# All eight accumulator banks as one set, in attention and in the MLP, with other durations in the planner

## The chip, the cores and the metric

The kernel runs on one core of one Trainium2 chip. The metric is the device time of one execution in microseconds; it is given as the median of several runs. One further execution was recorded by the hardware profiler, and every duration below comes from that recording.

Five engines work side by side: PE (TensorE, the matrix engine, with its weight loads shown as PEld), DVE (VectorE), ACT (ScalarE), POOL (GpSimd) and SP (SyncE, which here only issues DMAs). Each takes its own instructions in the order in which the program lists them. PE writes its results into accumulator banks (PSUM); there are eight of them, each 512 float32 wide on 128 partitions. DVE and ACT empty a bank; POOL works on SBUF only.

## The reference, cut to what matters

Attention over 4 batches, 8 heads, 768 positions, 64 dimensions: only pairs whose hash buckets agree take part (the signs of six random projections give the bucket), and the output feeds an MLP with a spatial gate.

```python
q_bucket = sum((q @ proj > 0) * 2**bit);  k_bucket likewise
scores   = where(q_bucket == k_bucket, q @ k.T / 8, -1e9)
attn     = exp(scores - max);  attn /= attn.sum() + 1e-9
x        = (attn @ v), heads side by side          # (4, 768, 512)
h        = gelu_tanh(x @ w_in);  u, v = halves of h # 512 wide each
v        = layer_norm(v) * g_ln
gated    = u * (w_sg @ v + b_sg)                   # w_sg mixes positions
out      = x + gated @ w_out
```

All products are float32; most are made of three or four reduced-precision products of a high and a low part.

## The kernel before

**Attention** runs over 16 pairs of heads; both heads of a pair stand on the two halves of the partitions. For each pair the program transposes q and k (`parts`, L476), projects them (`features`, L498), takes the row maxima of the scores (`largest`, product L518, maximum on DVE L525), turns the maxima into a shift (`shift`, DVE L533 and L534, product L540), and then, for each half of the positions, goes three times over two key tiles (`weigh`): scores L562, exponentials on ACT L568, their product with v L574 into one accumulator tile `av`, and running sums on POOL L583. `finish` adds the sums up over the partitions with a product against ones (L599), copies `av` out, and scales through small DMAs; its last DVE step is L620 and its result goes to DRAM as `xs`.

**The MLP** runs over four batches. For each: `hidden_v` (six tiles of 128 positions, product L757 in four groups of three matmuls each, then a chain of ACT and DVE steps L741 to L773), `hidden_u` (eight tiles, product L789, likewise four groups each, DVE L742 and L746), `gate` (eight tiles, product L807 in six groups each, DVE L810 and L814, ACT L815, POOL L818) and `project` (six tiles, product L833 in four groups each and a residual L838, copied out by ACT L842). In the first batch come `gate_weights`, twelve transposes of w_sg (PE L716, ACT L722, DVE L725), and `out_weights`: 16 jobs of seven DVE steps (L357 to L366) that make a high and a low part of w_out. The first `project` needs all sixteen. A "group" below is what the planner places as one piece: two matmuls of a pair of heads and more in attention, three matmuls in the MLP.

**What sets the order.** `Plan` holds a list of pieces of work with an engine, an assumed duration, a priority and the buffers they read and write. `order` runs through them once, at build time, with these assumed durations, and lists for each engine which piece comes after which. The chip then runs each engine's list in that order, whatever the true durations are. On PE the plan adds `TURN_PE` when the form of the array changes: "row" is a pair of products with 64 rows each (L518, L562), "col" a pair with 64 columns each (L574), None the full array.

**The banks.** In attention seven banks (`g0` to `g6`, `ps_tile`) are handed out by the planner, whichever is free first; the eighth is a ring of one, `av`. For `hidden_v` of the first batch the same seven are used. Then both pools are closed and the MLP has three rings: four banks `h` (hidden_v, hidden_u and the transposes of w_sg), two banks `vs` (gate), two banks `o` (project). A ring is used in turn: the fifth `h` tile waits until the first one has been read for the last time, which for hidden_v and hidden_u is DVE L746.

```python
ps_slots = {i: 0.0 for i in range(8 - NAV)}
st.av = ps_t.ring([P, 512], F32, "av", NAV)
return (po_ if tag == "o" else pm).ring(list(shape), F32, "ps_" + tag, bufs)
```

Of the kernel before, what the change touches and what calls it, by code (L numbers as in the profile page):

```python
# [24 lines left out]
AVP = 3.75  # L25
NAV = 1
# [7 lines left out]
class Plan:  # L34
# [8 lines left out]
    TURN_PE = 0.09  # L43
# [59 lines left out]
    def order(self):  # L103
# [120 lines left out]
def kernel(  # L224
# [179 lines left out]
    ps_t, ps_s = Pool("ps_t", "left", PSUM), Pool("ps_s", "left", PSUM)  # L404
    ftp = ps_t.pool.tile([P, 512], F32, tag="av", name="ftp", bufs=NAV)
# [12 lines left out]
    if True:  # L418
# [3 lines left out]
        ps_slots = {i: 0.0 for i in range(8 - NAV)}  # L422
# [14 lines left out]
        NPT = 16  # L437
# [29 lines left out]
        def parts(st, s, prio):  # L467

            hh, lo, raw, fac = st.hi[s], st.lo[s], st.raw[s], (SCALE, 1.0)[s]
            for hf in range(2):  # L470
# [19 lines left out]
        def features(st, s, prio):  # L490
            hh, lo, ft = st.hi[s], st.lo[s], st.ft[s]
            for hf in range(2):
# [11 lines left out]
                plan.add(PE, 0.58, prio, project, [(hh, hf), (lo, hf), (ft, hf)], [fp])  # L504
                plan.add(DVE, 0.67, prio, sign, [fp], [(ft, hf)])

        def largest(st, t, prio):
# [13 lines left out]
            for kh in range(2):  # L521
                plan.add(PE, 0.36, prio + 0.01 * kh, lambda kh=kh: mm(kh),
                         [(st.hi[0], hf), (st.hi[1], kh), (st.ft[0], hf), (st.ft[1], kh)], sc[kh], form="row")
                for j in range(2):
                    plan.add(DVE, 0.56, prio, lambda j=j, kh=kh: nc.vector.tensor_reduce(  # L525
                        mx()[:, kh, i, j:j + 1], sc[kh][j]()[:, :SH], axis=AX.X, op=ALU.max, negate=True),
                        [sc[kh][j]], [(mx, (kh, j, i))])
# [20 lines left out]
        def weigh(st, hf, k0, prio):  # L548

            cs, two = slice(hf * SH, (hf + 1) * SH), (k0, k0 + 1)  # L550
            if k0 == 0:
                st.av = ps_t.ring([P, 512], F32, "av", NAV)
                st.sum = [late.ring([P, SH], F32, "sum", 4) for _ in range(2)]
            av, sums = st.av, st.sum
# [16 lines left out]
            def product():
                for i, kt in enumerate(two):
                    for j in range(2):
                        nc.tensor.matmul(av()[row(j), :SH + 1], st.v()[:, j, kt, :], p[i][j](), start=(kt == 0), stop=(kt == NT - 1))  # L574

            plan.add(PE, 1.48, prio + AVP, product, p[0] + p[1] + [st.v], [av], form="col")
            for i, kt in enumerate(two):
# [3 lines left out]
                for j in range(2):  # L581
                    def add(j=j, i=i, e=e, first=p[0][j] if kt == 1 else sums[j]):
# [3 lines left out]
                             [sums[j]], port=True)  # L586

        def finish(st, hf, prio):
# [12 lines left out]
            plan.add(PE, 0.6, prio, total, sums, [tp])  # L601
# [50 lines left out]
        for n in range(NPAIR):  # L652
            for c in range(NT):
# [28 lines left out]
    def load_x(b, prio):  # L682
        r = []
        for c in range(NC):
# [7 lines left out]
            plan.add(ACT, 0.73, prio + c, lambda x=x, xh=xh: nc.scalar.copy(xh(), x()), [x], [xh])  # L692
            plan.add(M_["xl"], 1.76 if M_["xl"] == POOL else 0.87, prio + c, low, [x, xh], [xl])
# [9 lines left out]
    def gate_weights(prio):  # L703

        sg_v = w_sg.rearrange("(p t) s -> t p s", t=NT)
        for t in range(NT):
# [30 lines left out]
    def gelu2(ps, dst, n, prio, key=None):  # L737

        h2 = tile_of([P, FH], F32, "h2", 2)
        us = n / 960.0  # L740
        plan.add(ACT, us - 0.02, prio, lambda: nc.scalar.activation(h2()[:, :n], ps()[:, :n], AF.Square), [ps], [h2])  # L741
        plan.add(DVE, us + 0.07, prio, lambda: nc.vector.scalar_tensor_tensor(  # L742
            h2()[:, :n], h2()[:, :n], 1.0 / GA, ps()[:, :n], op0=ALU.add, op1=ALU.mult), [h2, ps], [h2])
        plan.add(ACT, us - 0.02, prio, lambda: nc.scalar.activation(h2()[:, :n], h2()[:, :n], AF.Tanh, scale=GC * GA),
# [4 lines left out]
    def hidden_v(xx, prio):  # L749
        zh, zl = tile_of([P, NT, FH], F32R, "zh", 1), tile_of([P, NT, FH], F32R, "zl", 1)  # L750
        for t in range(NT):
            ps, p0 = ps_of("h", 4), prio + t
            ts_ = slice(t * P, (t + 1) * P)
            for c, (xh, xl) in enumerate(xx):
# [4 lines left out]
                plan.add(PE, 0.65, p0 + 0.01 * c, mm, [xh, xl], [ps])  # L759
# [4 lines left out]
            plan.add(DVE, 0.6, p0, lambda y=y, st=st: V.bn_stats(st(), y()), [y], [st])  # L764
# [140 lines left out]
```

## Time and profile before

| what | value |
|---|---|
| time, three runs | 828.22, 830.72, 831.31 us |
| span of the profiled execution (first to last instruction) | 829.1 us |
| PE busy | 795.1 us, 96 % of the span, 5480 matmuls |
| DVE busy | 602.3 us, 73 % |
| POOL, ACT busy | 449.5 us, 54 %; 415.3 us, 50 % |
| granted clock of PE, mean | 0.988 |
| 16 DMA engines, mean | 74 GB/s |

The profiled execution is one more execution of the same program; its own time is its span, 829.1 us, which lies between the lowest run and the median. Attention fills the first 484 us, the MLP the rest. A page of the profile gives busy times per engine, then the same in 40 slices, the chain of work that ended last, and groups of equal instructions; other views show the waits, single instructions in order of time, and busy times in chosen stretches.

### The profile page before, as it was taken

What the parts mean: (1) busy time and instruction counts of PE and PEld (TensorE: products, weight loads), DVE (VectorE), ACT (ScalarE), POOL (GpSimd) and SP (SyncE); (2) the same over time, 40 slices, a digit from 0 to 9 for tenths busy, and PEclk for the clock granted to TensorE, in tenths of its full rate; (3) what the DMA queues carried; (4) which work ended last, traced back from release to release, by engine and by line L of the source; (5) the groups of instructions that cost most, each with busy time, mean ns of one, the idle gap of its engine ahead of it and who ended that gap; (6) DMA issues with size and microseconds to landing.
All of it is one profiled execution on the core that took longest, in us unless ns stands there. A gap on an engine that the chain in (4) does not pass through costs nothing.

```text
span 829.1 us, 15354 instructions
## 1 busy us (share of the span) xinstructions
PE 795.1 (96%) x5480; PEld 613.1 (74%) x5480; DVE 602.3 (73%) x1241; ACT 415.3 (50%) x926; POOL 449.5 (54%) x470
## 2 busy tenths in 40 slices
PE   6999999999999999999999997799799999999998
PEld 4766666666666676667667666698689889988996
DVE  6998889998989888998768538888943248516730
ACT  2456566565566656656665655613343135314411
POOL 1478887889868877787887862333105201601130
PEclk9899999999999999999999999799999999999999
DMA  5222441441442233133222011610024220131003
GB/s 152 51 51 74 107 122 34 111 127 36 113 110 57 73 97 91 34 110 78 60 58 60 21 40 41 223 45 25 27 83 134 82 90 1 39 106 47 1 1 127
DMA packets 99308, 60.94 MB, mean 74 GB/s; under 512 B 64288, under 2 KB 91040, under 8 KB 99232
## 3 DMA queue, kind: packets, MB, share of 16 engines
q1 hardware_dynamic: 97920, 56.94, 24.6%
q10 hardware_dynamic: 1312, 3.02, 1.0%
q8 instruction: 43, 0.70, 0.4%
q14 instruction: 33, 0.27, 0.2%
HBM read 47.16 MB, written 12.78 MB: 72 GB/s over the span
## 4 chain that ended last, share of the span: by engine, by line
PE 75%; DVE 19%; DMA 3%; issue 1%; ACT 1%; SPq 1%; DVEq 0%; ACTq 0%
PE g L562 15%; PE av L574 13%; PE ps_vs L807 12%; PE ps_o L833 8%; PE g L518 7%; PE ps_h L789 6%; DVE mx L525 5%; PE ps_h L757 4%; PE g L498 4%; PE g L476 2%; PE g L757 2%; PE g L540 1%; PE g L599 1%; PE ps_o L838 1%; DVE m L534 1%
## 5 line engine op out<-in xcount | busy, mean ns | idle before, releaser
L583 POOL TENSOR_TENSOR sum<-sum,p 128x384 f32<-128x384 f32 x256 | 260.7, 1049 | 61.1 <-ACT p L568 61.0
L525 DVE TENSOR_REDUCE mx<-g 128x1 f32<-128x384 f32 x384 | 187.7, 547 | 51.8 <-PE g L518 51.6
L568 ACT ACTIVATE p<-g 128x384 f32<-128x384 f32 x384 | 160.5, 494 | 104.9 <-PE g L562 97.4
L574 PE MATMUL av<-p,v 128*64 128x385 f32 x768 | 145.4, 500 | 0.0
L574 PEld LDWEIGHTS av<-p,v 128*64 128x64 f32 x768 | 46.6, 136 | 57.2 <-issue 53.6
L562 PE MATMUL g<-hq,hk 64*128 64x384 f32 x384 | 79.8, 389 | 2.4 <-DVE mx L525 2.4
L562 PEld LDWEIGHTS g<-hq,hk 64*128 64x128 f32 x384 | 39.5, 185 | 51.2 <-issue 26.7
L518 PE MATMUL g<-fk,fq 64*128 64x384 f32 x384 | 76.2, 360 | 0.5 <-DVE fk L501 0.2
L742 DVE SCALAR_TENSOR_TENSOR h<-h,ps_h 128x384 f32<-128x384 f32 (+1 forms) x50 | 29.1, 596 | 65.1 <-ACT h L741 64.8
L767 POOL TENSOR_TENSOR mv<-mv,epsr 128x1 f32<-128x1 f32 x24 | 14.8, 619 | 107.6 <-DVE mv L766 107.6
L518 PE MATMUL g<-hk,hq 64*128 64x384 f32 x384 | 71.6, 340 | 0.0
L583 POOL TENSOR_TENSOR sum<-p,p 128x384 f32<-128x384 f32 x64 | 64.3, 1026 | 10.4 <-ACT p L568 10.4
L562 PE MATMUL g<-hq,lk 64*128 64x384 f32 x384 | 68.9, 336 | 0.0
L562 PE MATMUL g<-lq,hk 64*128 64x384 f32 x384 | 68.7, 335 | 0.0
L562 PE MATMUL g<-fq,fk 64*128 64x384 f32 x384 | 68.6, 335 | 0.0
L833 PE MATMUL ps_o<-woh,gs 128*128 128x512 f32 x192 | 65.5, 402 | 0.0
L807 PE MATMUL ps_vs<-wgh,zl 128*128 128x384 f32 x192 | 64.3, 335 | 0.3 <-DVE zl L773 0.3
L807 PE MATMUL ps_vs<-wgh,zh 128*128 128x384 f32 x192 | 64.3, 335 | 0.0
L807 PE MATMUL ps_vs<-wgl,zh 128*128 128x384 f32 x192 | 64.2, 334 | 0.0
L818 POOL TENSOR_TENSOR gs<-gt,gs 128x384 fp32r<-128x384 f32 x32 | 33.3, 1043 | 55.0 <-ACT gs L815 55.0
L690 POOL TENSOR_TENSOR xl<-x,xh 128x768 fp32r<-128x768 f32 x16 | 30.1, 1890 | 47.6 <-ACT xh L692 38.3
L789 PE MATMUL ps_h<-xh,wih 128*128 128x384 f32 x128 | 44.7, 349 | 9.7 <-DVE y L746 8.2
(135 smaller groups left out, 1729.7 us busy)
## 6 DMA issues: line engine op xcount, KB each, us to landing
q<-in_q_dram SPq DMA_DIRECT2D x32, 192.0 KB
k<-in_k_dram SPq DMA_DIRECT2D x32, 192.0 KB
v<-in_v_dram SPq DMA_DIRECT2D x16, 384.0 KB
rs<-r SPq DMA_DIRECT2D x64, 96.0 KB
xs<-xt SPq DMA_DIRECT2D x32, 192.0 KB
x<-xs SPq DMA_DIRECT2D x16, 384.0 KB
rx<-xs SPq DMA_DIRECT2D x96, 64.0 KB
out_dram<-ob SPq DMA_DIRECT2D x24, 256.0 KB
```

Of the source, the lines that this page charges most:

```text
L498: nc.tensor.matmul(fp()[:, :SH], w[:, s, :], x()[:, cs], start=(i == 0), stop=(i == 2))
L518: nc.tensor.matmul(sc[kh][j]()[:, :SH], x[0]()[row(j), qs], x[1]()[row(j), kh * SH:(kh + 1) * SH], start=(n == 0), stop=(n == 1))
L525: plan.add(DVE, 0.56, prio, lambda j=j, kh=kh: nc.vector.tensor_reduce(mx()[:, kh, i, j:j + 1], sc[kh][j]()[:, :SH], axis=AX.X, op=ALU.max ...
L562: nc.tensor.matmul(sc[i][j]()[:, :SH], x()[row(j), ks], y()[row(j), cs], start=(n == 0), stop=(n == 3))
L568: plan.add(ACT, 0.53, prio, lambda i=i, j=j: nc.scalar.activation(p[i][j]()[:, :SH], sc[i][j]()[:, :SH], AF.Exp), [sc[i][j]], [p[i][j]])
L574: nc.tensor.matmul(av()[row(j), :SH + 1], st.v()[:, j, kt, :], p[i][j](), start=(kt == 0), stop=(kt == NT - 1))
L583: (nc.gpsimd if e == POOL else nc.vector).tensor_add(sums[j](), first()[:, :SH], p[i][j]()[:, :SH])
L757: nc.tensor.matmul(ps(), x()[:, ts_], w[:, c, FH:FF], start=(c == 0 and n == 0), stop=(c == NC - 1 and n == 2))
L789: nc.tensor.matmul(ps()[:, :SH], w[:, c, fs], x()[:, cs], start=(c == 0 and n == 0), stop=(c == NC - 1 and n == 2))
L807: nc.tensor.matmul(vp(), z()[:, t, fs], w()[:, t, cs], start=(t == 0 and n == 0), stop=(t == NT - 1 and n == 2))
L818: nc.gpsimd if e == POOL else nc.vector).tensor_sub(gl()[:, cs], gt(), gh()[:, cs].bitcast(F32)),
L833: nc.tensor.matmul(po(), a()[:, ts_], w()[:, f, :], start=(f == 0 and n == 0), stop=False)
```

## The change

One set of eight banks for everything: `av` is taken from `ps_tile` when the first product with v of a half is placed, and given back after it is copied out; the MLP's `ps_of` returns `ps_tile()` too. The rings `av`, `h`, `vs` and `o` and their pools are gone. The product with v becomes a function of its own, `weighted`; with `AVC` it is still placed once per two key tiles, at the same priority as before. There are 17 tiles for the exponentials in place of 16. The planner's assumed durations are replaced throughout (a selection is shown), and `TURN_PE` depends on the form that is entered. No instruction of the computation is added or taken away; the order on all engines is another.

```diff
-NAV = 1
+AVC = {0: (0, 2), 1: (2, 4), 2: (4, 6)}
...
-    TURN_PE = 0.09
+    TURN_PE = {"row": 0.2, "col": 0.14, "col32": 0.14, None: 0.14}
...
-        ps_slots = {i: 0.0 for i in range(8 - NAV)}
+        ps_slots = {i: 0.0 for i in range(8)}
...
-        NPT = 16
+        NPT = 17
...
             if k0 == 0:
-                st.av = ps_t.ring([P, 512], F32, "av", NAV)
-                st.sum = [late.ring([P, SH], F32, "sum", 4) for _ in range(2)]
-            av, sums = st.av, st.sum
+                st.sum, st.p = [late.ring([P, SH], F32, "sum", 4) for _ in range(2)], []
+            sums = st.sum
...
-            plan.add(PE, 1.48, prio + AVP, product, p[0] + p[1] + [st.v], [av], form="col")
+            st.p += p
...
+        def weighted(st, kts, prio):
+            if kts[0] == 0:
+                st.av = ps_tile()
+            av, p = st.av, st.p
+            def product():
+                for kt in kts:
+                    for j in range(2):
+                        nc.tensor.matmul(av()[row(j), :SH + 1], st.v()[:, j, kt, :], p[kt][j](), start=(kt == 0), stop=(kt == NT - 1))
+            plan.add(PE, 0.65 * len(kts), prio, product, [t for kt in kts for t in p[kt]] + [st.v], [av], form="col")
...
-            plan.add(PE, 0.6, prio, total, sums, [tp])
+            plan.add(PE, 0.375, prio, total, sums, [tp], form="col32")
...
     def ps_of(tag, bufs, shape=(P, FH)):
-        if pm is None:
-            return ps_tile()
-        return (po_ if tag == "o" else pm).ring(list(shape), F32, "ps_" + tag, bufs)
+        return ps_tile()
...
-    end = ps_s.close()
-    pm = Pool("pm", "right", PSUM, end)
-    end = ps_t.close(end)
-    po_ = Pool("po", "right", PSUM, end)
```

Other durations: the score product 0.71 to 0.692, an exponential 0.53 to 0.495, a maximum 0.56 to 0.55, a group of hidden_v 0.65 to 0.696, of gate 0.49 to 0.52, of project 0.65 to 0.685, DVE steps of the MLP by 0.08 to 0.1 longer.

How the lists move is shown at four places. `g` is a tile of the common set, `ps_h`, `ps_vs`, `ps_o` are the rings of before; the last number of a name tells one tile from another.

PE, where `hidden_v` of the second batch ends, before (from the last group of hidden_v):

```order
L757 MATMUL ps_h_8133<-wih,xl_7730 128x512
L807 MATMUL ps_vs_8165<-wgh_7617,zh_8094 128x384
L807 MATMUL ps_vs_8165<-wgl_7627,zh_8094 128x384
L807 MATMUL ps_vs_8165<-wgh_7617,zl_8109 128x384
L807 MATMUL ps_vs_8171<-wgh_7617,zh_8094 128x384
L807 MATMUL ps_vs_8171<-wgl_7627,zh_8094 128x384
L807 MATMUL ps_vs_8171<-wgh_7617,zl_8109 128x384
L789 MATMUL ps_h_8178<-xh_7590,wih 128x384
```

The same place after the change:

```order
L765 MATMUL g_1116_8103<-wih,xl_7738 128x512
L797 MATMUL g_1116_8131<-xh_7541,wih 128x384
L797 MATMUL g_1116_8131<-xl_7552,wih 128x384
L797 MATMUL g_1116_8131<-xh_7541,wil 128x384
L797 MATMUL g_1116_8131<-xh_7647,wih 128x384
```

Before, pieces of the gate of the second batch were put between hidden_v and hidden_u (2, 4 and 2 groups among the first 28 groups of hidden_u); now all 32 groups of hidden_u follow hidden_v, and then 24 groups of the gate.

PE, at the first `project` of the first batch, before:

```order
L789 MATMUL ps_h_8409<-xh_7696,wih 128x384
L789 MATMUL ps_h_8409<-xl_7730,wih 128x384
L789 MATMUL ps_h_8409<-xh_7696,wil 128x384
L833 MATMUL ps_o_8432<-woh_7588,gs_7793 128x512
L833 MATMUL ps_o_8432<-wol_7600,gs_7793 128x512
```

And after:

```order
L815 MATMUL g_1116_8496<-wgh_7572,zh_8099 128x384
L815 MATMUL g_1116_8496<-wgl_7614,zh_8099 128x384
L815 MATMUL g_1116_8496<-wgh_7572,zl_8113 128x384
L841 MATMUL g_1116_8529<-woh_7616,gs_7778 128x512
L841 MATMUL g_1116_8529<-wol_7635,gs_7778 128x512
```

When the first `project` begins, PE has now done all 32 groups of hidden_u and 24 of the gate of the second batch, where before it had done 28 and 8. The run lengths on PE around this are, before: 32 hidden_u, 12 transposes, 3 hidden_v, 48 gate, 21 hidden_v, 2 gate, 8 hidden_u, 4 gate, 4 hidden_u, 2 gate, 16 hidden_u, project; after: 32 hidden_u, 2 transposes, 1 hidden_v, 10 transposes, 4 hidden_v, 48 gate, 19 hidden_v, 32 hidden_u, 24 gate, project.

DVE, the last low parts of w_sg (`wgl`) and the jobs for w_out (`owy`, `owx`, `wol`), before:

```order
L366 SCALAR_TENSOR_TENSOR wol_7600<-owx_7649,woh_7588 128x128
L725 TENSOR_TENSOR wgl_7627<-ps_h_7684,wgh_7617 128x3x128
L357 TENSOR_SCALAR owy_7713<-ow_2_7676 128x128
L358 SCALAR_TENSOR_TENSOR owx_7716<-ow_2_7676,owy_7713 128x128
L360 SCALAR_TENSOR_TENSOR owx_7716<-owg_7706,owx_7716 128x128
L362 TENSOR_SCALAR owy_7713<-owx_7716 128x128
L363 SCALAR_TENSOR_TENSOR owy_7713<-ow_2_7676,owy_7713 128x128
L364 TENSOR_TENSOR owx_7716<-owx_7716,owy_7713 128x128
L725 TENSOR_TENSOR wgl_7627<-ps_h_7690,wgh_7617 128x3x128
```

And after:

```order
L358 SCALAR_TENSOR_TENSOR owx_7689<-ow_1_7612,owy_7685 128x128
L360 SCALAR_TENSOR_TENSOR owx_7689<-owg_7655,owx_7689 128x128
L362 TENSOR_SCALAR owy_7685<-owx_7689 128x128
L363 SCALAR_TENSOR_TENSOR owy_7685<-ow_1_7612,owy_7685 128x128
L364 TENSOR_TENSOR owx_7689<-owx_7689,owy_7685 128x128
L733 TENSOR_TENSOR wgl_7614<-g_1116_7658,wgh_7572 128x3x128
```

Behind the last row stand three more `wgl`, the last of the twelve. So the third job (`ow_2`) stood ahead of the last three `wgl` and now stands behind all of them.

PE, the sum over partitions (`finish`), in one of the middle pairs, before:

```order
L574 MATMUL av_3409<-p_160,v_2689 64x385
L599 MATMUL g_966_3558<-sum_3380,ones 32x192 x2
L599 MATMUL g_966_3558<-sum_3398,ones 32x192 x2
L498 MATMUL g_966_3573<-hq_4_3525,pwh 128x384
L498 MATMUL g_966_3573<-hq_4_3525,pwl 128x384
```

And after:

```order
L498 MATMUL g_1116_3563<-hk_4_3538,pwl 128x384
L498 MATMUL g_1116_3563<-lk_4_3549,pwh 128x384
L606 MATMUL g_1116_3570<-sum_3331,ones 32x192 x2
L606 MATMUL g_1116_3570<-sum_3346,ones 32x192 x2
L498 MATMUL g_1116_3578<-hk_4_3538,pwh 128x384
```

The sum stood at a place where the form changed anyway and now stands between two projections of the same form. Counted over the whole list of PE, the form changes at 303 places before and at 316 after.

More of the change, by code (lines that the diff above doesn't have):

```diff
@@ L163, in order @@
             if e == "PE":
-                work = g["c"] + (self.TURN_PE if g["form"] != form else 0.0)
+                work = g["c"] + (self.TURN_PE[g["form"]] if g["form"] != form else 0.0)
                 form = g["form"]
@@ L401, in close @@
             return [done]
-    ps_t, ps_s = Pool("ps_t", "left", PSUM), Pool("ps_s", "left", PSUM)
-    ftp = ps_t.pool.tile([P, 512], F32, tag="av", name="ftp", bufs=NAV)
+    ps_s = Pool("ps_s", "left", PSUM)
+    ftp = ps_s.pool.tile([P, 512], F32, tag="g0", name="ftp", bufs=1)
     for i in range(4):
@@ L564, in weigh @@
             for i, kt in enumerate(two):
-                plan.add(PE, 0.71, prio + 0.01 * i, lambda i=i: mm(i),
+                plan.add(PE, 0.692, prio + 0.01 * i, lambda i=i: mm(i),
                          [(x, hf) for x in (qh, ql, qf)] + [(x, kt // HT) for x in (kh, kl, kf)], sc[i], form="row")
                 for j in range(2):
-                    plan.add(ACT, 0.53, prio, lambda i=i, j=j: nc.scalar.activation(p[i][j]()[:, :SH], sc[i][j]()[:, :SH], AF.Exp),
+                    plan.add(ACT, 0.495, prio, lambda i=i, j=j: nc.scalar.activation(p[i][j]()[:, :SH], sc[i][j]()[:, :SH], AF.Exp),
                              [sc[i][j]], [p[i][j]])
[L571 to L574, printed above, removed]
-            plan.add(PE, 1.48, prio + AVP, product, p[0] + p[1] + [st.v], [av], form="col")
+            st.p += p
             for i, kt in enumerate(two):
@@ L658 @@
                 weigh(sts[n], hf, k0, 2 * g)
+                if c % HT in AVC:
+                    ks = AVC[c % HT]
+                    weighted(sts[n], range(*ks), 2 * g + AVP)
                 if c % HT == HT - 1:
@@ L690, in low @@
                 (nc.gpsimd if M_["xl"] == POOL else nc.vector).tensor_sub(xl(), x(), xh().bitcast(F32))
-            plan.add(ACT, 0.73, prio + c, lambda x=x, xh=xh: nc.scalar.copy(xh(), x()), [x], [xh])
-            plan.add(M_["xl"], 1.76 if M_["xl"] == POOL else 0.87, prio + c, low, [x, xh], [xl])
+            plan.add(ACT, 0.83, prio + c, lambda x=x, xh=xh: nc.scalar.copy(xh(), x()), [x], [xh])
+            plan.add(M_["xl"], 1.88 if M_["xl"] == POOL else 0.87, prio + c, low, [x, xh], [xl])
             r.append((xh, xl))
@@ L763, in hidden_v @@
             V = nc.vector
-            plan.add(DVE, 0.6, p0, lambda y=y, st=st: V.bn_stats(st(), y()), [y], [st])
+            plan.add(DVE, 0.69, p0, lambda y=y, st=st: V.bn_stats(st(), y()), [y], [st])
             plan.add(DVE, 0.08, p0, lambda st=st, mv=mv: V.bn_aggr(mv()[:, 0:2], st()), [st], [mv])
@@ L806, in mm @@
                         for n, (z, w) in enumerate(((zh, wgh), (zh, wgl), (zl, wgh))):
-                            nc.tensor.matmul(vp(), z()[:, t, fs], w()[:, t, cs], start=(t == 0 and n == 0),
+                            nc.tensor.matmul(vp()[:, :SH], z()[:, t, fs], w()[:, t, cs], start=(t == 0 and n == 0),
                                              stop=(t == NT - 1 and n == 2))
-                    plan.add(PE, 0.49, p0 + 0.01 * t, mm, [(zh, t), (zl, t), wgh, wgl], [vp])
-                plan.add(DVE, 0.47, p0, lambda vp=vp, gt=gt, cs=cs: nc.vector.tensor_add(gt(), vp(), b_bc()[:, cs]),
+                    plan.add(PE, 0.52, p0 + 0.01 * t, mm, [(zh, t), (zl, t), wgh, wgl], [vp])
+                plan.add(DVE, 0.56, p0, lambda vp=vp, gt=gt, cs=cs: nc.vector.tensor_add(gt(), vp()[:, :SH], b_bc()[:, cs]),
                          [vp, b_bc], [gt])
                 e = M_["gm"]
-                plan.add(e, 0.96 if e == POOL else 0.47, p0, lambda gt=gt, f=f, cs=cs, e=e: (
+                plan.add(e, 1.03 if e == POOL else 0.56, p0, lambda gt=gt, f=f, cs=cs, e=e: (
                     nc.gpsimd if e == POOL else nc.vector).tensor_mul(gt(), gt(), us[f]()[:, cs]), [gt, (us[f], hf)], [gt], port=True)
-                plan.add(ACT, 0.4, p0, lambda gt=gt, gh=gh, cs=cs: nc.scalar.copy(gh()[:, cs], gt()), [gt], [(gh, hf)])
+                plan.add(ACT, 0.51, p0, lambda gt=gt, gh=gh, cs=cs: nc.scalar.copy(gh()[:, cs], gt()), [gt], [(gh, hf)])
                 e = M_["gl"]
-                plan.add(e, 0.96 if e == POOL else 0.47, p0, lambda gt=gt, gh=gh, gl=gl, cs=cs, e=e: (
+                plan.add(e, 1.03 if e == POOL else 0.56, p0, lambda gt=gt, gh=gh, gl=gl, cs=cs, e=e: (
                     nc.gpsimd if e == POOL else nc.vector).tensor_sub(gl()[:, cs], gt(), gh()[:, cs].bitcast(F32)),
@@ L833, in mm @@
                         nc.tensor.matmul(po(), a()[:, ts_], w()[:, f, :], start=(f == 0 and n == 0), stop=False)
-                plan.add(PE, 0.65, p0 + 0.01 * f, mm, [(gh, hf), (gl, hf), woh, wol], [po])
+                plan.add(PE, 0.685, p0 + 0.01 * f, mm, [(gh, hf), (gl, hf), woh, wol], [po])
             def residual(rx=rx, po=po):
@@ L841, in project @@
             plan.add(PE, 0.43, p0 + 0.1, residual, [rx], [po])
-            plan.add(ACT, 0.5, p0, lambda ob=ob, po=po: nc.scalar.copy(ob(), po()), [po], [ob])
+            plan.add(ACT, 0.59, p0, lambda ob=ob, po=po: nc.scalar.copy(ob(), po()), [po], [ob])
             dma(p0, 0.73, lambda eng, ob=ob, t=t: eng.dma_start(ov[:, t, :], ob()), [ob])
@@ L872 @@
     plan.run(tc)
-    for p in (b3, b2, b1, po_, pm):
+    for p in (b3, b2, b1, ps_s):
         p.pool.release()
```

30 lines of the change are left out of this document (15 added, 15 removed).

## The prediction

> **What bounds the kernel now.** I read the page first, then the busy times by stage, then PE's waits, then the engine that PE waits for.
>
> ```profile
> PE 795.1 (96%) x5480; PEld 613.1 (74%) x5480; DVE 602.3 (73%) x1241; ACT 415.3 (50%) x926; POOL 449.5 (54%) x470
> ```
>
> PE is the bound: 795.1 of 829.1 us. No instruction comes or goes, so what can change is PE's idle time (34 us), the time that it loses at changes of form, and its clock.
>
> ```profile
> 0.00:40.00 40.00, 31.89 (x182) 24.55 (x184) 32.56 (x100) 13.35 (x28) 9.80 (x24) 0.91 0.42 106
> 40.00:486.00 446.00, 438.57 (x3625) 296.42 (x3623) 371.74 (x715) 275.44 (x659) 355.96 (x357) 1.00 0.29 76
> 486.00:542.00 56.00, 46.82 (x226) 39.23 (x223) 45.47 (x96) 30.30 (x60) 18.60 (x20) 0.91 0.32 106
> 542.00:609.00 67.00, 61.37 (x316) 56.61 (x315) 60.10 (x162) 24.12 (x50) 17.95 (x27) 0.97 0.10 32
> 609.00:829.00 220.00, 216.43 (x1139) 196.26 (x1137) 92.48 (x171) 72.09 (x130) 47.21 (x44) 1.00 0.21 66
> ```
>
> Columns: stretch and its length, busy time of PE, PEld, DVE, ACT, POOL, granted clock, DMA. PE's idle time is 8.1 us at the start, 7.4 in 446 us of attention, 9.2 and 5.6 in the first part of the MLP, and 3.6 after 609, which is the last copy and store. So the MLP's first 123 us hold 15 of the 34 us, and there DVE is busy 106 of 123 us. The waits of PE there:
>
> ```profile
> PE ps_h L789 <- DVE y L746: 8.2, 5, 3.9
> PE ps_h L716 <- DVE wgl L725: 2.8, 3, 2.3
> PE ps_h L716 <- DVE u L746: 1.9, 2, 1.0
> PE ps_h L789 <- DVE u L746: 1.6, 1, 1.6
> ```
>
> (in total, times, longest). All are PE waiting for one of the four `h` banks that DVE has not read out. The rows:
>
> ```profile
> 506.71 0.44 PE L789 MATMUL ps_h<-xh,wih 128*128 128x384 f32 x1 [1.01 <-DVE y L746]
> 510.90 0.45 PE L789 MATMUL ps_h<-xh,wih 128*128 128x384 f32 x1 [1.83 <-DVE y L746]
> 517.00 0.44 PE L789 MATMUL ps_h<-xh,wih 128*128 128x384 f32 x1 [1.58 <-DVE u L746]
> 598.41 0.69 PE L789 MATMUL ps_h<-xh,wih 128*128 128x384 f32 x1 [3.85 <-DVE y L746]
> ```
>
> **The change, part by part.** Durations of a group on PE, from the chain of work:
>
> ```profile
> 541.61 24.97 PE ps_vs L807 x144
> 670.05 16.80 PE ps_h L757 x72
> 686.84 8.33 PE ps_h L789 x48
> ```
>
> Three matmuls are a group: 0.52 us for the gate (24.97/48), 0.70 for hidden_v (16.80/24), 0.52 for hidden_u (8.33/16); a tile of hidden_u is four groups, 2.08 us.
>
> *Up to the gate of the first batch (541.6).* With eight banks the three waits at 506, 510 and 517 (4.4 us) go: hidden_u begins one tile ahead of the first of them, DVE has read the last tile of hidden_v when the second ends (510.9), and until then four tiles of hidden_u and what is left of hidden_v need no more than eight banks. What is late next is DVE, for the gate needs the twelfth `wgl`. DVE's list from its first MLP step on:
>
> ```profile
> 489.60 0.69 DVE L742 SCALAR_TENSOR_TENSOR h<-h,g 128x512 f32<-128x512 f32 x1 [7.28 <-ACT h L741]
> 537.87 0.22 DVE L357 TENSOR_SCALAR owy<-ow 128x128 int32<-128x128 int32 x1
> 538.51 1.73 DVE L360 SCALAR_TENSOR_TENSOR owx<-owg,owx 128x128 f32<-128x128 f32 x1
> 541.08 1.48 DVE L725 TENSOR_TENSOR wgl<-ps_h,wgh 128x384 fp32r<-128x384 f32 x3
> L742 DVE SCALAR_TENSOR_TENSOR h<-h,ps_h 128x384 f32<-128x384 f32 x8 | 4.3, 546 | 1.3 <-ACT h L741 1.3
> L746 DVE SCALAR_TENSOR_TENSOR u<-h,ps_h 128x384 f32<-128x384 f32 x8 | 4.3, 550 | 1.3 <-ACT h L744 1.2
> L700 DVE COPY b_bc<-gs 128x768 f32<-128x768 f32 x1 | 0.9, 935 | 1.1 <-DMA gs<-in_moe_w_sg_dram 1.1
> ```
>
> (the last three: groups from 515 to 543). The third job's six steps stand ahead of the last three `wgl` before, and not after: 541.08 less 537.87, where the first of them starts, is 3.2 us, 1.73 of it one step that took long; I take 3.0. Of the 3.7 us that DVE idles in these three groups, the 2.6 behind ACT exist because PE sent the tiles late; I take 1.6. So the gate starts at 541.6 − 3.0 − 1.6 = 537.0. Ends: 535 (the rest of the 3.7 us goes too) and 541.6 (another step is as long in its place, nothing moves).
>
> *From the gate to `project`.* Five groups of hidden_v now stand ahead of the gate, in place of three. On PE: 48 gate groups, 537.0 + 25.0 = 562.0; 19 of hidden_v, 575.3; then hidden_u, 2.08 a tile. DVE sets what follows:
>
> ```profile
> 568.41 0.68 DVE L742 SCALAR_TENSOR_TENSOR h<-h,ps_h 128x512 f32<-128x512 f32 x1
> 597.67 0.68 DVE L746 SCALAR_TENSOR_TENSOR y<-h,ps_h 128x512 f32<-128x512 f32 x1
> 604.38 0.74 DVE L773 SCALAR_TENSOR_TENSOR zl<-y,mv,zh 128x512 fp32r<-128x512 f32 x1
> 608.68 0.28 DVE L366 SCALAR_TENSOR_TENSOR wol<-owx,woh 128x128 fp32r<-128x128 f32 x1
> L360 DVE SCALAR_TENSOR_TENSOR owx<-owg,owx 128x128 f32<-128x128 f32 x8 | 2.6, 326 | 0.2
> L746 DVE SCALAR_TENSOR_TENSOR u<-h,ps_h 128x384 f32<-128x384 f32 x4 | 2.2, 546 | 0.0
> ```
>
> DVE has no gap worth naming from its first step for the second batch (568.41, 1.8 us behind the gate's last matmul) to the sixth tile's release (597.67 + 0.6), its last `zl` (605.1) and the last `wol` (608.9). After the change that first step comes at 562.0 + 1.8 = 563.8. Up to the sixth release DVE's list holds the same steps, with one hidden_u step less: 29.9 − 0.6 = 29.3, so 593.1. Of eight banks five to eight are then in use: tiles 1 to 7 of hidden_u fit (575.3 + 7 × 2.08 = 589.9), the eighth waits 3.2 us and ends at 595.2. The 24 gate groups (12.5 us) need the first bank of hidden_u, for which DVE has eight steps behind the sixth release, 3.7 us at the means of these groups (596.8, a wait of 1.6), and after five groups the last `zl` (605.1 − 568.4 = 36.7 behind the first step, 600.5, a wait of 1.1): they end at 596.8 + 12.5 + 1.1 = 610.4. The last `wol` has more ahead of it than before: one job (seven steps of up to 0.33, about 1.7 as they overlap), two tiles' steps of hidden_u (2 × 0.9) and two gate steps (1.0): 563.8 + 40.5 + 4.5 = 608.8, so it does not hold `project` up, which started at 608.7 before. By 610.4 PE has done 16 gate groups (8.3 us) and four of hidden_u (2.1) more: gain 8.3 + 2.1 − 1.7 = **8.7 us**, which contains the 4.6 above. Ends: 4.1, if the gate still starts at 541.6, and 11, if it starts at 535. After 609 PE never waits, so the moved gate pieces of batches three and four cost and give nothing; PE's own 216 us cover DVE's 92.
>
> *Form changes.* One run of projections between other forms:
>
> ```profile
> 120.09 0.45 PE L498 MATMUL g<-hk,pwh 128*128 128x384 f32 x1
> 120.37 0.34 PE L498 MATMUL g<-hk,pwl 128*128 128x384 f32 x1
> 120.55 0.35 PE L498 MATMUL g<-lk,pwh 128*128 128x384 f32 x1
> 121.09 0.34 PE L498 MATMUL g<-lk,pwh 128*128 128x384 f32 x1
> 121.36 0.44 PE L562 MATMUL g<-hq,hk 64*128 64x384 f32 x2
> ```
>
> Start to start is 0.18 inside; behind a change it is 0.28 and ahead of one 0.27, so a change costs 0.1 on either side, 0.2. 316 in place of 303 is 13 × 0.2 = **2.6 us lost**, all on PE with nothing to hide it.
>
> *The bank of `av`, 17 exponentials, other durations in attention.* Between the copy of `av` and the next first product the bank is free for others, and in its life one of eight is held as before. What waits there now:
>
> ```profile
> PE g L540 <- DVE m L534: 3.5, 6, 1.1
> PE g L562 <- DVE mx L525: 2.4, 5, 0.7
> PE g L476 <- DVE mx L525: 1.5, 1, 1.5
> ```
>
> That is 7.4 us in 32 half pairs. Counted in groups, the shift product L540 stands at most places of the new list as far behind its maxima as in the old one, at some further, so I take no change. Ends: −6 (nearly all goes) and +6 (as much again). The start is DVE's chain of maxima in both lists: 0, ±2.
>
> Sum: 829.1 − 8.7 + 2.6 = 823.0 against the profiled execution. The median of the runs is 1.6 above that execution, by which it would be 824.6; I say **823**.
>
> A rule bears on the waits that are left. In the trace the clock fell to half although no wait was over 2.3 us:
>
> ```profile
> 525.00:530.00 5.00, 2.81 (x16) 2.24 (x15) 4.02 (x10) 4.31 (x10) 1.95 (x2) 1.00 0.55 194
> 530.00:535.00 5.00, 3.35 (x14) 2.19 (x12) 4.61 (x9) 2.62 (x6) 3.61 (x3) 0.50 0.55 175
> ```
>
> The Trainium skill, "TensorE: Matmul & The Clock Gate", section "Why this matters for your kernels", asks for no idle gap above about 3 us and puts the return to half clock behind one idle window. By that rule the short waits left ahead of the gate would not slow PE: the five groups of hidden_v there could be up to 3.5 us shorter, but as DVE ends that stretch the sum would be at most 1 us less. The rows above differ from the rule, and I keep theirs.
>
> **The rivals.**
> 1. *DVE's dates don't move.* DVE is 86 % busy there, and its gaps may come from DMA and ACT. Then the gate starts at 541.6, PE waits later instead: gain 4.1 − 2.6 = 1.5, 827.6. For it: the step of 1.73 us, which may come again elsewhere. Against it: one job less ahead of the last `wgl`.
> 2. *More waits in attention, slower.* `av` takes its bank from the set that scores and maxima use, so a score product may find a bank still with the maxima. One such wait is 0.5 us (2.4/5), and the half pairs are 32. From 20 more of them on the gain of 6.1 has become a loss of 4: at one for each half pair, 0.5 × 32 = 16, the time is 839. Against it: the set has eight.
> 3. *More banks give nothing*, since PE only reaches the same DVE dates earlier, in both stretches: 829.1 + 2.6 = 831.7. The Trainium skill's same page, section "HAM oscillation", tells of a kernel in which double-buffering PSUM "gave no further gain". Against it: 10.4 us of PE work that needs no late `wol` now stand ahead of `project`.
> 4. *Attention's waits fall as well*: 823.0 − 6 = 817.0.
>
> **How the numbers follow.** A change under 0.5 % (4 us) can't be told from none. Forecast 0.56, from 818 to 827 with its ends; rival 4 0.12; rival 1 0.15 (no change); rival 3 0.07 (no change); rival 2 0.10 (slower). Faster 0.69, same 0.21, slower 0.10. The range 816 to 830 leaves out rival 2, most of rival 3 and the low tail, together 0.2.
>
> **What would show it.** Right: no wait of L797 (hidden_u, was L789) between 500 and 520; the 48 gate groups start near 537; one wait for DVE near 590; the first `project` near 610; PE idle under 10 us between 486 and 610. Wrong: the gate at 541 or later, `project` later than 615, or PE idle above 12 us between 40 and 484.

## The result, and the profile after

| | time, median (lowest to highest) | profiled span |
|---|---|---|
| before | 830.32 us (828.22 to 831.31), 4 runs | 829.1 us |
| after | 819.93 us (818.07 to 820.99), 4 runs | 818.7 us |

The ratio is 0.9867, with a 95 % interval of 0.985 to 0.9885: 10.4 us less. A time is some 1.8 us longer than the span of the same execution: the profiled one after took 820.49 us, and its span is 818.7. Times are compared with times below, and spans with spans. First the page, then the busy times in the same five stretches as before (the columns are the same; the last stretch ends at 818), then PE's waits from 486 to 609 (us in total, times, longest):

```profile
PE 794.2 (97%) x5480; PEld 611.7 (75%) x5480; DVE 591.5 (72%) x1241; ACT 414.9 (51%) x926; POOL 447.2 (55%) x471
```

```profile
0.00:40.00 40.00, 32.97 (x202) 25.40 (x204) 31.20 (x96) 12.96 (x29) 12.41 (x27) 0.91 0.41 99
40.00:486.00 446.00, 444.58 (x3644) 298.90 (x3640) 368.19 (x727) 278.92 (x665) 357.63 (x359) 1.00 0.29 77
486.00:542.00 56.00, 51.93 (x274) 47.14 (x267) 47.33 (x104) 28.91 (x58) 16.58 (x19) 0.94 0.35 114
542.00:609.00 67.00, 58.71 (x296) 54.44 (x295) 60.92 (x157) 28.42 (x56) 22.05 (x28) 0.95 0.15 46
609.00:818.00 209.00, 206.04 (x1079) 185.81 (x1078) 83.83 (x160) 65.70 (x120) 38.53 (x40) 1.00 0.19 62
```

```profile
PE g L797 <- DVE y L754: 3.5, 2, 3.1
PE g L815 <- DVE zl L781: 3.4, 1, 3.4
PE g L765 <- DVE u L754: 1.5, 1, 1.5
PE g L815 <- DVE u L754: 1.3, 1, 1.3
PE g L724 <- DVE u L754: 1.0, 1, 1.0
```

PE's work is the same (795.1 and 794.2 us) and its idle time fell from 34 to 24.5 us. In attention (40 to 486) hardly any is left, 1.4 us where there were 7.4. From 486 to 542 it is 4.1 (9.2 before). But from 542 to 609 it *rose*, from 5.6 to 8.3.

When each stage begins is read from the matmuls of one line ("first to last start", us). Before: product with v, gate, `project`:

```profile
L574 PE MATMUL av<-p,v x768: 487/487/538, 35.3 to 486.1; 128*64 128x385 f32 x192
L807 PE MATMUL ps_vs<-wgh,zh x192: 334/334/441, 541.4 to 805.5; 128*128 128x384 f32 x192
L833 PE MATMUL ps_o<-woh,gs x192: 387/395/478, 608.5 to 824.6; 128*128 128x512 f32 x192
```

After:

```profile
L591 PE MATMUL g<-p,v x768: 487/487/538, 30.9 to 478.1; 128*64 128x385 f32 x192
L815 PE MATMUL g<-wgh,zh x192: 333/334/522, 528.7 to 795.1; 128*128 128x384 f32 x192
L841 PE MATMUL g<-woh,gs x192: 387/394/478, 608.6 to 814.2; 128*128 128x512 f32 x192
```

Attention's last product with v starts 8.0 us earlier, the gate 12.7 us earlier, and `project` at the same time, with 10.4 us more of PE's work (16 gate groups, 4 of hidden_u) done by then. So by 608 the gain is 10.4 us: 8.0 from attention and only some 2.4 from the MLP, of which 4.7 had been gained up to the gate and 2.3 given back behind it. The experiments ask whether that account tells what each part is worth. It does not.

### The profile page after: what moved, and what is told of

Read it like the earlier page. It is cut to its first block, busy times and chain, and to the rows that moved or that the text cites. A ratio compares the mean times of both kernels' runs of the same rounds, so it can differ in the third digit from the quotient of the medians.

```text
span 818.7 us, 15328 instructions
## 1 busy us (share of the span) xinstructions
PE 794.2 (97%) x5480; PEld 611.7 (75%) x5480; DVE 591.5 (72%) x1241; ACT 414.9 (51%) x926; POOL 447.2 (55%) x471
## 4 chain that ended last, share of the span: by engine, by line
PE 81%; DVE 13%; DMA 3%; issue 1%; SPq 1%; ACT 1%; POOL 0%; ACTq 0%; DVEq 0%
PE g L561 18%; PE g L591 16%; PE g L815 9%; PE g L518 9%; PE g L841 8%; PE g L765 5%; PE g L498 4%; PE g L797 4%; PE g L476 2%; PE g L540 2%; PE g L606 2%; DVE mx L525 1%; PE g L846 1%; DMA ow<-in_moe_w_out_dram 1%; DVE h L750 1%
## 5 line engine op out<-in xcount | busy, mean ns | idle before, releaser
L591 PE MATMUL g<-p,v 128*64 128x385 f32 x768 | 145.2, 499 | 0.0
L591 PEld LDWEIGHTS g<-p,v 128*64 128x64 f32 x768 | 46.6, 136 | 57.5 <-issue 55.9
L750 DVE SCALAR_TENSOR_TENSOR h<-h,g 128x384 f32<-128x384 f32 (+1 forms) x56 | 32.7, 605 | 65.1 <-ACT h L749 64.9
L561 PE MATMUL g<-hq,hk 64*128 64x384 f32 x384 | 76.1, 391 | 0.3 <-DVE mx L525 0.3
L815 PE MATMUL g<-wgh,zl 128*128 128x384 f32 x192 | 64.8, 338 | 3.4 <-DVE zl L781 3.4
L815 PE MATMUL g<-wgh,zh 128*128 128x384 f32 x192 | 65.2, 339 | 1.3 <-DVE u L754 1.3
L841 PE MATMUL g<-woh,gs 128*128 128x512 f32 x192 | 65.5, 402 | 0.0
L815 PE MATMUL g<-wgl,zh 128*128 128x384 f32 x192 | 64.9, 338 | 0.0
L818 DVE TENSOR_TENSOR gt<-g,b_bc 128x384 f32<-128x384 f32 x32 | 17.7, 554 | 55.2 <-PE g L815 35.5
L628 POOL TENSOR_TENSOR xt<-xt,e 128x384 f32<-128x384 f32 x32 | 32.4, 1011 | 33.0 <-ACT e L626 17.5
```

Of the source, the lines that this page charges most:

```text
L561: nc.tensor.matmul(sc[i][j]()[:, :SH], x()[row(j), ks], y()[row(j), cs], start=(n == 0), stop=(n == 3))
L815: nc.tensor.matmul(vp()[:, :SH], z()[:, t, fs], w()[:, t, cs], start=(t == 0 and n == 0), stop=(t == NT - 1 and n == 2))
L841: nc.tensor.matmul(po(), a()[:, ts_], w()[:, f, :], start=(f == 0 and n == 0), stop=False)
```

## Experiments: which part gives the time

Four kernels first, each with one part of the change.

**Banks alone.** The kernel before, with one set of eight banks everywhere, the old durations and `TURN_PE`.

```diff
-        ps_slots = {i: 0.0 for i in range(8 - NAV)}
+        ps_slots = {i: 0.0 for i in range(8)}
...
-                st.av = ps_t.ring([P, 512], F32, "av", NAV)
+                st.av = ps_tile()
...
-        if pm is None:
-            return ps_tile()
-        return (po_ if tag == "o" else pm).ring(list(shape), F32, "ps_" + tag, bufs)
+        return ps_tile()
```

> The old durations stay; the eight banks become one set (av from it too, the MLP too), 16 tiles for the exponentials. Theory (attention's gain of 7 us comes from the list that the new durations make, the banks gain only in the MLP, 3 us): last product with v starts within 1.5 us of 485, PE's waits in attention stay near 7 us, time 826 to 829. Rival (the banks make attention's gain): last product with v near 478, time 819 to 823. Form changes in its list: 307.

Measured: 830.01 us, ratio 0.9996 (0.9981 to 1.0012): nothing. The rival fails, and the theory's time does too: the 3 us that it had the banks gain in the MLP did not come under the old durations.

**Durations alone.** The changed kernel with the old banks (seven and `av`; rings of four, two, two) and 16 tiles.

> The new durations and prices of a change of form, with the old banks (seven and one for av, then rings of 4, 2 and 2) and 16 tiles. Theory: attention gains as in the changed kernel, last product with v near 478, MLP as before: time 822 to 825. Rival (the banks do it): 829 to 833, for the list has 317 changes of form against 303, 2.8 us at 0.2 each.

Measured: 829.0 us, ratio 0.9978 (0.9966 to 0.999), some 1.8 us less than before (0.8 to 2.8). That is the rival's time; the theory's 822 to 825 was missed.

**Rings in the MLP.** The changed kernel, with the rings back behind attention.

```diff
-        return ps_tile()
+        if pm is None:
+            return ps_tile()
+        return (po_ if tag == "o" else pm).ring(list(shape), F32, "ps_" + tag, bufs)
...
+    end = ps_s.close()
+    pm = Pool("pm", "right", PSUM, end)
+    po_ = Pool("po", "right", PSUM, end)
```

> The changed kernel with the MLP's rings of 4, 2 and 2 banks put back after attention; attention's list is the same one to the first hidden_v. Theory: the three waits of hidden_u for h banks near 500 are back (4 us) and the MLP's gain of 3.3 us is gone: 822 to 825. Rival (DVE's dates set the MLP, the banks nothing): 819 to 821.

Measured: 828.48 us, ratio 0.9969 (0.995 to 0.9988), 8.6 us more than the changed kernel: neither the theory's 822 to 825 nor the rival's 819 to 821. PE's longest entry of waits from 486 to 609 is hidden_u waiting for one of the four `h` banks again:

```profile
PE ps_h L799 <- DVE u L756: 8.6, 3, 4.3
```

The product with v in these three, banks alone, durations alone, rings in the MLP:

```profile
L573 PE MATMUL g<-p,v x768: 486/487/538, 36.2 to 487.1; 128*64 128x385 f32 x192
```

```profile
L592 PE MATMUL av<-p,v x768: 486/487/538, 33.9 to 485.0; 128*64 128x385 f32 x192
```

```profile
L591 PE MATMUL g<-p,v x768: 486/487/539, 30.6 to 477.5; 128*64 128x385 f32 x192
```

Neither banks (+1.0) nor durations (−1.1) alone move the end of attention; both together do (−8.6). And the third kernel has the whole of that lead and ends some 2 us ahead of before.

**A bank of its own for `av`, and eight shared in the MLP.** The opposite of the last one.

```diff
+        ps_slots, av_slots, mlp_slots = Some(range(7)), Some([7]), Some(range(8))
...
-                st.av = ps_tile()
+                st.av = ps_tile(av_slots)
...
-        return ps_tile()
+        return ps_tile(mlp_slots)
```

(`Some` is a view of one table of eight banks that shows only the given ones.)

> The changed kernel, but in attention av keeps a bank of its own and seven are shared (the planner's durations, the 17 tiles, the eight shared banks of the MLP stay); 321 changes of form. Theory S: attention's 8 us come from sharing av's bank under the new durations, since the durations alone gave 1 us: the last product with v is near 484, and the MLP's banks give 4 to 8 us: 821 to 825. Rival T: the 17th tile or the luck of the list gives it: the last product with v near 477, and 819 to 821.

Measured: 820.58 us, ratio 0.9877 (0.9844 to 0.991). Product with v, gate, `project`, and PE's two longest waits from 486 to 609:

```profile
L609 PE MATMUL g<-p,v x768: 487/487/539, 33.3 to 486.5; 128*64 128x385 f32 x192
L833 PE MATMUL g<-wgh,zh x192: 334/334/422, 533.7 to 793.4; 128*128 128x384 f32 x192
L859 PE MATMUL g<-woh,gs x192: 387/393/481, 612.2 to 812.5; 128*128 128x512 f32 x192
```

```profile
PE g L742 <- DVE wgl L751: 3.1, 2, 1.6
PE g L815 <- DVE y L772: 1.9, 1, 1.9
```

Attention ends as late as before (486.5), and yet the kernel is as fast as the changed one. Theory S was right that sharing `av`'s bank is what ends attention early, and near on the place (484 for 486.5); its time, 821 to 825, was just missed. Rival T has the time (819 to 821) but not the place (477). The four kernels with the new durations:

| | rings in the MLP | eight banks in the MLP |
|---|---|---|
| `av` with its own bank | 829.0 | 820.6 |
| `av` from the common set | 828.5 | 819.9 |

The MLP's banks are worth 8.4 and 8.6 us; sharing `av`'s bank 0.5 and 0.7, which can't be told from nothing, although it ends attention 8 us earlier. (The planner makes a new list for each, so a difference holds that as well.) And the MLP's 8.4 and 8.6 hold under the new durations only: under the old ones eight banks everywhere gave nothing (banks alone).

**Sixteen tiles.** The changed kernel with `NPT = 16`; the first two kernels of this part had 16, the others 17.

> The changed kernel with 16 tiles for the exponentials in place of 17; all engines' lists stay the same. If no product with v and no exponential waits for a tile: the last product with v at 477, 820 us. If the 17th tile is what makes attention 8 us shorter: the last product near 484.

Measured: 820.51 us, ratio 0.9879 (0.9844 to 0.9913). The tile gives nothing; the last product with v comes 2.3 us later, not 8:

```profile
L591 PE MATMUL g<-p,v x768: 487/487/538, 31.9 to 480.4; 128*64 128x385 f32 x192
```

In the profiled executions, in which PE, DVE and ACT run the same lists, these 2.3 us are not made up again: `project` starts 2.0 us later (610.6), and the span is 2.0 us longer (820.7). The medians differ by 0.6 only, so this is one pair of executions and no more.

## Experiments: where attention's lead goes

Busy times from 478 to 600 (length, PE, PEld, DVE, ACT, POOL, clock, DMA): before, after, and with `av`'s own bank:

```profile
478.00:600.00 122.00, 107.19 (x557) 91.59 (x554) 98.19 (x232) 54.96 (x112) 43.56 (x53) 0.95 0.21 68
```

```profile
478.00:600.00 122.00, 109.64 (x559) 98.33 (x556) 104.71 (x248) 58.32 (x116) 44.45 (x52) 0.96 0.24 77
```

```profile
478.00:600.00 122.00, 115.16 (x621) 102.11 (x620) 100.58 (x241) 61.62 (x125) 46.64 (x55) 0.97 0.24 74
```

With the lead PE does 109.6 us of work there, without it 115.2. DVE works 86 % of the time with it, 82 % without.

What the lead turns into shows from 478 to 620, by when all four kernels with the new durations are at `project`. With rings, `av` with its own bank and from the common set; then with eight banks, the same two:

```profile
478.00:620.00 142.00, 127.72 (x646) 110.90 (x643) 106.20 (x256) 60.80 (x124) 41.73 (x53) 0.94 0.24 76
478.00:620.00 142.00, 125.64 (x605) 112.87 (x606) 107.78 (x260) 58.99 (x117) 36.92 (x48) 0.89 0.22 70
478.00:620.00 142.00, 135.16 (x729) 120.45 (x727) 112.00 (x268) 67.33 (x136) 50.27 (x58) 0.98 0.24 75
478.00:620.00 142.00, 129.64 (x656) 116.34 (x653) 111.67 (x268) 62.62 (x124) 44.85 (x53) 0.95 0.24 77
```

With rings PE idles 14.3 us there without the lead and 16.4 with it; with eight banks 6.8 and 12.4. The granted clock is lower with the lead as well, 0.89 for 0.94 and 0.95 for 0.98, which over 142 us is an estimate of 7 and 4 us. Idle time and clock together take about what attention had won, or a little more. In part this is DVE: in the changed kernel PE is at the second batch's hidden_u 7.0 us earlier than with `av`'s own bank (567.0 for 574.0), but DVE's sixth release comes 5.1 us earlier (584.8 for 589.9) and its last `wol` 5.3 (606.8 for 612.1). The order on PE differs too (24 groups of the gate ahead of `project` for 34), and no run separates the two.

Two kernels took work off DVE without touching the order: three of the seven DVE steps of each w_out job are left out, 48 in all, so the last product is computed from an incomplete w_out.

```diff
+        full = CW > 128
-        vec(lambda: sts(xf(), g(), LEAST * LEAST, ...
+        vec(lambda: full and sts(xf(), g(), LEAST * LEAST, ...
...
-        vec(lambda: V.tensor_add(xf(), xf(), yf()), [x, y], [x])
+        vec(lambda: full and V.tensor_add(xf(), xf(), yf()), [x, y], [x])
```

> The changed kernel, with three of the seven DVE steps of each of the 16 w_out jobs left out (the one that zeroes small values, the scaled low word, the sum of both): 48 steps, 17.0 us of DVE between 516 and 607. Every engine's list is otherwise the same, to the instruction. The output's last product is computed from an incomplete w_out. Theory D: what PE waits for between 486 and 610 are DVE's dates, so the 10 us of waits there mostly go and the first project comes 6 to 10 us earlier: 812 us (810 to 814). Rival L: the jobs' own chain (one buffer for the load of w_out, a step on POOL, a step on ACT) sets the dates: under 2 us, 818 to 820.

> The kernel before with the same 48 DVE steps left out, its lists otherwise the same. Theory D: its waits in the MLP's first part (15 us) are for DVE's dates as well, and it gains as much as the changed kernel does, 6 to 10 us: 822 us, so that the banks are worth the same 10 us with DVE relieved. Rival R: with four banks the hidden_u tiles wait for the chain of ACT and DVE steps of one tile, whatever DVE has besides: under 4 us, 827, and the changed kernel is then 14 us or more ahead.

Measured: the changed kernel 812.55 us, 7.4 less; the kernel before 823.57, 6.9 less (ratios to before 0.9776, 0.9749 to 0.9803, and 0.9916, 0.9884 to 0.9947). PE's longest waits from 486 to 609, changed kernel and kernel before, both with the lighter jobs:

```profile
PE g L816 <- DVE u L755: 2.2, 1, 2.2
PE g L766 <- DVE u L755: 1.5, 1, 1.5
```

```profile
PE ps_h L790 <- DVE y L747: 4.8, 3, 1.9
```

Theory D holds in both: in the changed kernel the first `project` comes 7.9 us earlier (600.7), and the waits of 3.1 and 3.4 us are gone with nothing moved but DVE's dates. They did not "mostly go", though: PE's waits there are 5.7 us in all, of 12.3. The rival, that with four banks hidden_u waits for one tile's chain whatever DVE has besides, fails on the time; the waits between 505 and 517 that it was about did stay (the 4.8 us hold two of them, as long as before). DVE relieved, the two kernels are 11.0 us apart, much as without (10.4).

**The add on POOL.** Nothing is left out; one of a job's DVE steps goes to POOL.

```diff
-        vec(lambda: V.tensor_add(xf(), xf(), yf()), [x, y], [x])
+        plan.add("POOL", 0.14 + CW / 512, when(), lambda: nc.gpsimd.tensor_add(xf(), xf(), yf()), [x, y], [x])
```

(for the jobs of w_out only)

> The changed kernel with the same add on POOL, and nothing else. Theory D: 817.5 (816 to 819). Rival: 820 or more.

Measured: 814.74 us, ratio 0.981 (0.9776 to 0.9843): 5.2 less than the changed kernel, twice what theory D's rate gave. More than the adds went: other steps of DVE, which are the same in both, became shorter. Counted as in the last section, steps that stood behind POOL are longer by 2.4 us in all, where it was 7.9. DVE's groups from 500 to 610 (busy us, mean ns, idle before), changed kernel, then this one:

```profile
L781 DVE SCALAR_TENSOR_TENSOR zl<-y,mv,zh 128x512 fp32r<-128x512 f32 x9 | 8.2, 917 | 0.9 <-ACT zh L779 0.9
L357 DVE TENSOR_SCALAR owy<-ow 128x128 int32<-128x128 int32 x16 | 6.7, 420 | 2.8 <-DMA ow<-in_moe_w_out_dram 2.8
```

```profile
L784 DVE SCALAR_TENSOR_TENSOR zl<-y,mv,zh 128x512 fp32r<-128x512 f32 x9 | 6.7, 745 | 0.9 <-ACT zh L782 0.9
L357 DVE TENSOR_SCALAR owy<-ow 128x128 int32<-128x128 int32 x16 | 5.1, 316 | 0.4 <-DMA ow<-in_moe_w_out_dram 0.2
```

## Experiments: fewer products with v

**One per half**, in place of three.

```diff
-AVC = {0: (0, 2), 1: (2, 4), 2: (4, 6)}
+AVC = {2: (0, 6)}
```

> The changed kernel with one product with v per half in place of three (all six key tiles in one piece): 180 changes of form in place of 316, and the av bank is held for a third of the time. By the price of 0.2 us each change that is 27 us less on PE. Theory: PE is the bound and a change costs 0.2, so 27 us less but for new waits, since 12 of the 17 exponential tiles are then held until the product: 795 to 812. Rival (the exponentials' tiles bind: the scores of the next half wait for the product of the last): 820 to 850.

Measured: 811.81 us, ratio 0.9778 (0.9754 to 0.9803), with 180 changes of form in place of 316. The page, and the longest entry of PE's waits from 40 to 476:

```profile
PE 777.4 (96%) x5480; PEld 624.9 (77%) x5480; DVE 595.1 (73%) x1241; ACT 410.7 (51%) x926; POOL 447.3 (55%) x471
```

```profile
PE g L561 <- DVE mx L525: 9.2, 10, 3.3
```

PE's busy time is 16.8 us less than after, but 9.8 of that came back as idle time, most of it in waits for maxima (0.3 us after). The time is at the upper end of the theory's range. The tiles of the exponentials, which the rival had in mind, did not bind: among ACT's waits from 40 to 476 is none of an exponential for a product with v.

**Two per half** (`AVC = {1: (0, 3), 2: (3, 6)}`).

> The changed kernel with the product with v placed twice per half (three key tiles each) in place of three times: 268 changes of form in place of 316. By the price of 0.2 us alone: 48 x 0.2 = 9.6 us less, 810. By the run with one product per half, where 136 changes fewer gave 8 us because waits for maxima took the rest: 48/136 of 8 = 3 us, 817.

Measured: 816.4 us, ratio 0.9828 (0.9797 to 0.9859). The interpolated 817 was near, the price alone (810) was not. PE's busy time is 786.4 us, 7.8 less for 48 changes fewer.

**One per half, and `av` with its own bank.**

> One product per half, with a bank of its own for av in attention and eight shared banks in the MLP; 161 changes of form. If sharing av's bank is worth nothing in the end (0.7 us of 8 were left in the runs so far), this is as fast as one product with the shared bank: 812 (809 to 815). If sharing matters more where av is held only during one product (the bank is free for scores the rest of the half), the waits for maxima grow and it is slower: 816 or more.

Measured: 828.84 us, ratio 0.9977 (0.9956 to 0.9998). So sharing `av`'s bank, worth nothing with three products, is worth 17 us with one (828.84 against 811.81). From the first product of a half to the end of the copy of `av`, the bank is held 10.5 us with three products and 4.6 with one (medians over the halves, from the trace), and a half takes 14.3 and 14.0 us on average. That fits the second sentence of the expectation; but the waits for maxima did not grow as it said, the loss is spread over attention and the MLP, and its cause is not settled. The last product with v, shared and own:

```profile
L591 PE MATMUL g<-p,v x768: 486/487/538, 38.4 to 476.9; 128*64 128x385 f32 x192
```

```profile
L609 PE MATMUL g<-p,v x768: 487/487/848, 38.6 to 488.6; 128*64 128x385 f32 x192
```

**One per half, shared banks, and the add on POOL**: the two parts that gained, together.

> One product per half with shared banks, and the add of each of the 16 w_out jobs moved from DVE to POOL: some 5.4 us off DVE in the MLP's first part. Theory D: 17.0 us less on DVE gave 7.4, so 5.4 give 2.3: 809.5 (808 to 811). Rival: each add on POOL lengthens a job's chain by two waits and makes DVE's SBUF steps wait behind POOL; no gain, 812 to 814.

Measured: 806.54 us, ratio 0.9708 (0.9676 to 0.9739), 5.3 less than without the move and again more than theory D's rate gave (808 to 811). This is the fastest version, 13.4 us below the changed kernel.

## Why the prediction was right, and where its steps failed

The forecast of 823 came within 3.1 us of the median, and the changed kernel lies in the range. The sum itself is a span, 823.0, and is to be held against the span of 818.7: it gave 6.1 us, and 10.4 came. Nearly all of the 4.3 us between lies in one place: the new durations alone, form changes included, made the kernel some 1.8 us faster, where the sum had 2.6 lost to form changes and nothing gained. Step by step:

- *The MLP's term, −8.7.* Its size is what the table above gives, 8.4 and 8.6, in kernels of which attention ends alike. The account of the changed kernel itself (2.4) hides it behind attention's lead. Its two parts below were both off, so that the size is right is in part luck; and the prediction did not say that the term needs the new durations.
- *The gate's start.* The waits of hidden_u between 500 and 520 are gone. The gate started at 528.75; without attention's 8.0 that is 4.7 us earlier than before, where 4.6 was predicted. But the subtraction is no test: with `av`'s own bank, where attention ends as before, the gate starts at 533.7, 7.7 us earlier and beyond the end of the range (535). The step was too small.
- *From the gate to `project`.* This step failed. 73.4 us were predicted (537.0 to 610.4), 79.9 came. The hidden_v part held: DVE's sixth release came 28.4 us behind its first step (29.3 predicted):

```profile
557.08 0.67 DVE L750 SCALAR_TENSOR_TENSOR h<-h,g 128x512 f32<-128x512 f32 x1
584.81 0.68 DVE L754 SCALAR_TENSOR_TENSOR y<-h,g 128x512 f32<-128x512 f32 x1
596.60 2.29 DVE L781 SCALAR_TENSOR_TENSOR zl<-y,mv,zh 128x512 fp32r<-128x512 f32 x1
```

  The last `zl` was taken from the old list, 36.7 us behind the first step; it ended 41.8 behind it. In the new list DVE has hidden_u's steps and further jobs between the sixth release and that `zl`, and the `zl` itself took 1.5 us more than its kind. The gate groups of the second batch waited 3.4 us for it instead of 1.1. With `av`'s own bank the stretch is 78.5 us (533.7 to 612.2), too long as well, though 10 more groups of the gate (5.2 us) stand in it. PE's idle time between 486 and 609, 12.4 us, broke the bound of 10 set for it. That the first `project` came at 608.6, near the 610 named, is luck, the sum of two errors: 8.2 us early at the gate, nearly all of it attention's lead, and 6.5 late behind it.
- *Attention's waits, 0 (−6 to +6).* Also failed. The last product with v came 8.0 us earlier. PE's idle time from 40 to 486 fell by 6.0 us, the very end of the range, and by 1.1 before 40; the waits of the shift product fell from 3.5 to 0.9 us, and the first product with v came at 30.9 instead of 35.3. Counting how far that product stands behind its maxima in the two lists did not tell this. In the time the term was still near 0 (0.5 and 0.7 us in the table): the lead reaches the MLP, and there PE waits more and has the lower clock.
- *Form changes, +2.6.* The count is right. With 136 changes fewer PE's busy time fell by 16.8 us, 0.12 a change, and with 48 fewer by 7.8, 0.16 a change, so 13 would be 1.6 to 2.1 rather than 2.6. In the time the loss does not show: with the durations alone the form changes at 317 places, and that kernel is faster than before. As a forecast of a time the price alone is no good: with two and with one product waits took much of what it promised.
- *The rivals.* Rival 1, the gate at 541.6 still, did not come (528.7, and 533.7 with `av`'s own bank). Rival 4 named attention's gain, but not that it would be lost later. Rival 2, slower by waits for a bank in attention, did not come. Rival 3 (PE only reaches the same DVE dates earlier) failed for the banks, which are worth 8.4 and 8.6 us; taking 17 us from DVE gave 7 us in both kernels.

What stays open: why the lead turns into waits and a lower clock in the MLP. DVE carried some 5 of the 8 us to its late dates, and the order on PE is another; with the same lists on PE, DVE and ACT (sixteen tiles) 2.3 us were not made up again. DVE relieved, the changed kernel ends its products with v some 7 us ahead of before and is 11.0 us ahead in all, no more than when it is not relieved. A kernel with lighter jobs and `av`'s own bank, which would tell whether the lead is then worth something, was not run.

## What to carry to other kernels

A lead that one stage wins need not be worth anything at the end: here 8 us became 0.5 to 0.7. Put a part of a change on its own, and its opposite as well, before a stage's dates are booked as its gain; and look whether a part needs another one, as the banks here needed the new durations. Where an engine is busy for nearly 90 % of a stretch, take its dates from the new list to the last step that somebody waits for, not only to the middle. Sharing a bank was worth nothing here where it is held for nearly three quarters of the time, and 17 us where it is held for a third; that the holding time is the cause was not shown.

## What the runs showed of the hardware

**DVE steps that stood behind POOL.** The step of 1.73 us that the prediction met at 538.51 ended at 540.24, 0.15 us after an instruction of POOL that had begun before it; the `zl` of 2.29 us above is the same (it began at 596.60, POOL ended at 598.34). POOL's instructions, before and after:

```profile
538.17 1.92 POOL L690 TENSOR_TENSOR xl<-x,xh 128x768 fp32r<-128x768 f32 x1 [1.78 <-ACT xh L692]
```

```profile
596.40 1.94 POOL L698 TENSOR_TENSOR xl<-x,xh 128x768 fp32r<-128x768 f32 x1
```

In the changed kernel nine DVE steps from 486 to 610 took over 0.3 us more than the median of their line and shape, 7.9 us together, and each overlapped an instruction of POOL that ended 0.08 to 0.55 us before it did. In the trace such waiting counts as busy time of DVE. In the first 478 us the same count gives 42 us before and 31 after. It does not set the time by itself: with one product and `av`'s own bank it is 17, in a kernel no faster than before. The Trainium skill, "SBUF — State Buffer", section "SBUF: two separate sides", says that a DVE instruction with two inputs in SBUF, or in a mode that uses two ports, and an instruction of GpSimd that reads SBUF share one pair of ports, and that the one that comes second waits for the whole of the first. The rows agree.

**The clock behind a short wait.** The granted clock (the third figure from the end) fell after the waits of 3.1 us that ended at 585 and of 3.4 us that ended at 599, as the rule that the prediction takes from the Trainium skill has it, but also from 515 to 520, where no wait of PE was longer than 1.5 us:

```profile
515.00:520.00 5.00, 2.22 (x8) 1.38 (x8) 4.93 (x13) 4.17 (x11) 2.26 (x1) 0.79 0.88 314
585.00:590.00 5.00, 3.73 (x12) 3.22 (x12) 4.79 (x14) 3.83 (x7) 2.25 (x3) 0.66 0.09 26
600.00:603.00 3.00, 3.00 (x11) 3.00 (x11) 2.90 (x10) 1.70 (x4) 0.00 (x0) 0.50 0.30 111
```

So a row of short waits can cost half the clock too, here as in the kernel before.
